# The third expert's rows asked for in the third step, the first expert's in the eighth

## The chip, the cores and the metric

One core of one Trainium2 chip runs the program. A time is device microseconds (us) of one execution; lower is better. The kernel before was timed three times, and one more execution was profiled.

## The reference

Three layers run one after the other on 3072 tokens of 384 numbers, all in float32.

```
attn:  state = alpha * state + k v^T ; y = q state          (4 x 8 heads, 768 steps, 48 wide)
moe:   h = x @ w_in ; g = h * cos(h) ; x = g @ w_out        (384 -> 2048 -> 384)
moe2:  a token with x @ w_skip > 0 goes to the expert e with the largest x @ w_gate, of 8:
       out = x + gate * (relu(x @ w1[e]) @ w2[e])           (384 -> 1024 -> 384)
       every other token: out = x
```

The change concerns the third layer, the second MoE, alone.

## The kernel before

**Stages.** Attention and the first MoE run together, in 256 half-steps, until about 588 us. The last group of tokens is routed, and then the second MoE runs, from about 602 us to the end. In it every expert has 276 slots in a table in HBM, `xs`; a slot holds a token's 384 numbers, its 8 gate logits and its row number (394 words). Tokens were scattered to their slots before.

**The second MoE.** One loop (L1008) runs over steps F = 0 to 65, eight steps for each expert (e = F // 8, f = F % 8). A step is one block of 128 of the expert's 1024 hidden numbers: `e_L1` makes the block h by nine matmuls (L958), ScalarE takes `ha` = relu(h) rounded (L961), VectorE takes `hb`, the rest of it (L962); `e_L2`, two steps later, adds the block's nine matmuls into three accumulators (L975). The tile `h` has two buffers, so the first layer of step F must wait until `hb` of step F - 2 is done.

**Loads of rows.** `e_load(e)` (L937) fetches the 276 slots of expert e into a tile `xg`: 92 partitions, three rows of 394 words on each, 425 KB, as one DMA on SyncE's queue (L939). `xg` has three buffers. An expert's rows are read three times:

- `e_T(e, k)`: three TensorE transposes each (L948), in three successive steps of the expert before it, so that the first layer can begin. For expert 1 in steps F = 5, 6 and 7, for expert 2 in steps F = 12, 13 and 14. Expert 0 needs none: its transposed rows were made in another way before the loop.
- `e_gate(e)`: the gate of its 276 tokens, five small operations on VectorE (L103, L105, L107, L109, L110) with one exponential on ScalarE (L106) in the midst. For expert 0 in step F = 9.
- `e_Y(e, j)`: VectorE multiplies the output by the gate and adds the token (L991), and GpSimd scatters it (L994). For expert 0 in steps 10, 11 and 12.

The loads of the first three experts are asked for in steps 0 (expert 1), 4 (expert 0) and 7 (expert 2); the later ones at the end of each expert, step 15 for expert 3 and so on. Here a load is called by its expert: load 1, load 0, load 2.

**Weights.** In each step `e_weights` asks for one piece of weights (L270 or L273, 384 KB on 128 partitions, tile `st`) six steps ahead of its use, and converts the piece that is due: ScalarE takes the rounded part (L287), VectorE the rest (L288). These DMAs go through the same queue of SyncE, between the loads of rows. `st` has six buffers, so SyncE waits for the conversion in the same step before it asks for the next piece.

**Order.** From half-step 246 on the order on every engine is the order of the program text (`tc.manual_schedule()`, L817); no scheduler moves anything. Inside a step it is: first layer, second layer, loads and pieces, gate, transposes of the next expert, output of the last one.

Of the kernel before, what the change touches and what calls it, by code (L numbers as in the profile page):

```python
# [19 lines left out]
DFF, E, EFF = 2048, 8, 1024  # L20
# [210 lines left out]
def linear_attention_moe_kernel(outer, tc, qk, al, v, w_in, w_out, w1, w2, idw, cst, csti, fill, q0, k0, v0, alpha0, out):  # L231
# [416 lines left out]
    with ExitStack() as order_ctx:  # L648
# [161 lines left out]
        for t in range(0, END + 2 * LAG + 1):  # L810
# [7 lines left out]
            if t >= 0:  # L818
                F, odd = divmod(t, 2)
# [84 lines left out]
        def flags1():  # L904
            ok = keep.tile([PR, 2], F32, name="ok2")
            sm = keep.tile([PR, 3], F32, name="sm")
            nc.vector.tensor_reduce(out=sm[:, 0:1], in_=amax, axis=AX.X, op=ALU.max)
            nc.vector.tensor_reduce(out=sm[:, 1:2], in_=T_all.rearrange("p n a b -> p (n a b)"), axis=AX.X, op=ALU.min)
            nc.vector.tensor_reduce(out=sm[:, 2:3], in_=run[0:PR, :], axis=AX.X, op=ALU.max)
            nc.vector.tensor_scalar(out=ok[:, 0:1], in0=sm[:, 0:1], scalar1=0.0, scalar2=None, op0=ALU.is_le)  # L910
            nc.vector.scalar_tensor_tensor(
                out=ok[:, 0:1], in0=sm[:, 1:2], scalar=T_MIN, in1=ok[:, 0:1], op0=ALU.is_ge, op1=ALU.mult
            )
            nc.vector.scalar_tensor_tensor(
                out=ok[:, 0:1], in0=sm[:, 2:3], scalar=float(CAP), in1=ok[:, 0:1], op0=ALU.is_le, op1=ALU.mult
            )
            return ok

        def flags2(ok):
            fp = tps()  # L920
            nc.tensor.matmul(fp[0:1, 0:1], ok[:, 0:1], ones_f, start=True, stop=True)
            nc.vector.tensor_scalar(
                out=flag, in0=fp[0:1, 0:1], scalar1=-1.0, scalar2=float(PR), op0=ALU.mult, op1=ALU.add
            )
# [12 lines left out]
        def e_load(e):  # L937
            x = p2.tile([ET, NJ, RW], F32, tag="xg", name="xg", bufs=3)
            nc.sync.dma_start(out=x, in_=xs[CAP * e:CAP * e + CAP, :].rearrange("(j p) d -> p j d", p=ET))  # L939
            XG[e] = x  # L940

        def e_gate(e):
            GW[e] = _gate(nc, p2, ET, NJ, XG[e][:, :, DM:DM + E], bufs=3)

        def e_T(e, k):
            pt = tps()
            for j in range(NJ):
                nc.tensor.transpose(pt[:, ET * j:ET * j + ET], XG[e][:, j, 128 * k:128 * k + 128], ident[0:ET, 0:ET])  # L948
            split_T(e, k, pt[:, 0:CAP])

        def e_L1(e, f):
            h = psh.tile([P, 512], F32, tag="h", name="h2")[:, 0:CAP]
            w = ew[e, 1]
            a, b = XT[e]
            fs = slice(128 * f, 128 * f + 128)
            k9 = [(i, x, k) for k in range(3) for i, x in ((0, a), (0, b), (1, a))]
            for n, (i, x, k) in enumerate(k9):
                nc.tensor.matmul(h, w[:, i, k, fs], x[:, k, :], start=(n == 0), stop=(n == 8))  # L958
            ha = ph[0].tile([P, CAP], F32R, tag="ha", name="ha")
            hb = ph[0].tile([P, CAP], F32R, tag="hb", name="hb")  # L960
            nc.scalar.activation(out=ha, in_=h, func=ACTF.Relu)  # L961
            nc.vector.scalar_tensor_tensor(  # L962
                out=hb, in0=h, scalar=0.0, in1=ha.bitcast(F32), op0=ALU.max, op1=ALU.subtract
            )
            H2[e, f] = (ha, hb)

        def e_L2(e, f):
            if f == 0:
                ACC[e] = [ps.tile([P, 512], F32, tag=f"acc{j}", name=f"acc{j}")[:, 0:CAP] for j in range(3)]
            w = ew[e, 2]  # L970
            a, b = H2.pop((e, f))
            for j in range(3):
                js = slice(128 * j, 128 * j + 128)
                for i, (wi, x) in enumerate(((0, a), (0, b), (1, a))):
                    nc.tensor.matmul(ACC[e][j], w[:, wi, f, js], x, start=(f == 0 and i == 0), stop=(f == NF2 - 1 and i == 2))  # L975
            if f == NF2 - 1:
                yt = p2.tile([P, 3, CAP], F32, tag="yt", name="yt")
                for j in range(3):
                    if j == 1:
                        nc.vector.tensor_copy(yt[:, j, :], ACC[e][j])  # L980
                    else:
                        nc.scalar.activation(out=yt[:, j, :], in_=ACC[e][j], func=ACTF.Copy)
                ACC[e] = yt

        def e_Y(e, j):
            pt = tps()[0:ET, 0:DM]
            for k in range(3):
                nc.tensor.transpose(pt[:, 128 * k:128 * k + 128], ACC[e][:, k, ET * j:ET * j + ET], ident)
            res = p3.tile([ET, DM], F32, tag="res", name="res")
            x = XG[e]  # L990
            nc.vector.scalar_tensor_tensor(  # L991
                out=res, in0=pt, scalar=GW[e][:, j, :], in1=x[:, j, 0:DM], op0=ALU.mult, op1=ALU.add
            )
            ins = nc.gpsimd.indirect_dma_start(  # L994
                out=out[:, :], out_offset=bass.IndirectOffsetOnAxis(ap=x[:, j, RW - 1:RW].bitcast(I32), axis=0),
                in_=res, in_offset=None, bounds_check=NTOK - 1, oob_is_err=False,
            )
            tc.declare_no_dep(ins.ins, group="rows", reason="every token has one slot")
            tc.add_to_no_dep_group("rows", ins.ins)
# [3 lines left out]
        def e_weights(i):  # L1003
            for p in pieces[i:i + 1] + pieces[i + WA:i + WA + 1]:
                next(p, None)

        tot2 = E * NF2
        for F in range(tot2 + 2):  # L1008
            e, f = divmod(F, NF2)
            if F < tot2:  # L1010
                e_L1(e, f)
            if F >= 2:
                e_L2((F - 2) // NF2, (F - 2) % NF2)
            if F < tot2:
                if F == 0:
                    e_load(1)
                e_weights(F + 4)
                if F == 4:
                    e_load(0)
                if f == FG and e or F == FG0:  # L1020
                    e_gate(e if F != FG0 else 0)
                if e + 1 < E:
                    if 0 <= f - (TF if e else TF0) < 3:
                        e_T(e + 1, f - (TF if e else TF0))
                if e >= 1 and YF <= f < YF + 3:
                    e_Y(e - 1, f - YF)
                if f == 7 and e + 2 < E:
                    e_load(e + 2)
            if F == FL1:
                ok = flags1()  # L1030
            if F == FL2:
                flags2(ok)
# [92 lines left out]
```

## Time and profile before

| | us |
|---|---|
| median of 3 runs | 785.15 |
| lowest and highest | 783.29, 785.52 |
| the profiled execution | 781.24 |
| its span, first to last instruction | 779.5 |
| busy: TensorE matmul (PE) | 742.0 (95%) |
| busy: VectorE (DVE) | 515.4 (66%) |
| busy: ScalarE (ACT) | 420.5 (54%) |
| busy: GpSimd (POOL) | 213.1 (27%) |

A row of a timeline gives the start in us, the time from the start of the first to the end of the last of the instructions that it merges, the engine, the line, the operation with what it writes and reads, how many, and in brackets how long the engine had stood idle before and what ended that. SPq is SyncE's queue, where only the issue of a DMA is seen, not its transfer. In the windows PEclk is the granted share of TensorE's 2.4 GHz: 1.00 is that level, 0.50 is 1.2 GHz.

### The profile page before, as it was taken

To read this page: it belongs to the slowest core of one execution; us is meant where nothing else is said; L and a number is where in the kernel's file an instruction comes from. 1 tells how busy PE (TensorE), PEld (TensorE's weight loads), DVE (VectorE), ACT (ScalarE), POOL (GpSimd) and SP (SyncE) were. 2 spreads that over 40 slices of the span, in tenths; PEclk is the share of its full clock that TensorE was granted. 3 is DMA by queue.
4 is the path that set the end of the run, shared out by engine and by line. 5 is a ranking of instruction groups with operands and counts; after the bars stand their busy time and mean duration, and the time that the engine had idled before them with its cause. 6 is when DMAs were issued, how large, how long until landed. Compare 5 with 4: busy or idle time off the path is not lost.

```text
span 779.5 us, 13544 instructions
## 1 busy us (share of the span) xinstructions
PE 742.0 (95%) x5033; PEld 725.8 (93%) x5033; DVE 515.4 (66%) x1088; ACT 420.5 (54%) x877; POOL 213.1 (27%) x217
## 2 busy tenths in 40 slices
PE   6689999999999999999999999999999989999995
PEld 4689899989999999999999999999998989999994
DVE  5889999986676656667756544444444667777772
ACT  3789996454454454455445445535554545555551
POOL 3003324232524224222422322232342021111112
PEclk7979999999999999999999999999999999999998
DMA  9858772421233222213322210102033766666621
GB/s 274 272 186 267 232 251 85 147 94 34 72 115 99 84 95 85 68 52 114 100 84 90 75 60 16 51 22 87 31 100 108 195 164 195 196 182 188 199 65 27
DMA packets 53217, 94.77 MB, mean 122 GB/s; under 512 B 7950, under 2 KB 39265, under 8 KB 53048
## 3 DMA queue, kind: packets, MB, share of 16 engines
q1 hardware_dynamic: 47528, 88.82, 37.5%
q0 software_dynamic: 4992, 4.80, 2.1%
q8 instruction: 41, 0.67, 0.4%
q10 hardware_dynamic: 624, 0.21, 0.1%
q14 instruction: 32, 0.26, 0.1%
HBM read 82.03 MB, written 16.43 MB: 126 GB/s over the span
## 4 chain that ended last, share of the span: by engine, by line
PE 60%; issue 16%; DVE 6%; POOL 3%; DMA 2%; ACT 1%; POOLq 0%; SPq 0%; ACTq 0%
PE acc L570 24%; PE h L535 22%; PE sc L438 4%; POOL out L994 3%; PE y L448 2%; PE y L451 2%; DMA xg<-xs 2%; PE u L494 1%; PE y L454 1%; DVE w L398 1%; PE h L958 1%; DVE w L409 1%; PE pt L429 1%; PE wg L323 1%; DVE n L539 1%
## 5 line engine op out<-in xcount | busy, mean ns | idle before, releaser
L556 POOL TENSOR_TENSOR gl<-n,gh 128x384 fp32r<-128x384 f32 x127 | 140.2, 1104 | 334.9 <-ACT gh L554 247.8
L535 PE MATMUL h<-x,win_h 128*128 128x384 f32 x768 | 204.6, 347 | 7.7 <-ACT x L474 5.8
L535 PEld LDWEIGHTS h<-x,win_h 128*128 128x128 f32 x768 | 137.8, 191 | 9.4 <-ACT x L474 6.0
L570 PE MATMUL acc<-wout_h,gh 128*128 128x394 f32 x384 | 136.7, 356 | 0.0
L570 PE MATMUL acc<-wout_h,gl 128*128 128x394 f32 x384 | 132.0, 344 | 0.4 <-POOL gl L556 0.4
L570 PE MATMUL acc<-wout_l,gh 128*128 128x394 f32 x384 | 132.2, 344 | 0.0
L535 PE MATMUL h<-x,win_l 128*128 128x384 f32 x384 | 130.8, 341 | 0.0
L546 ACT ACTIVATE n<-n,lims 128x384 f32<-128x384 f32 x128 | 78.9, 616 | 89.1 <-DVE n L539 89.0
L539 DVE SCALAR_TENSOR_TENSOR n<-n,h 128x384 f32<-128x384 int32 x128 | 70.1, 548 | 83.7 <-ACT n L538 82.8
L554 ACT ACTIVATE gh<-n 128x384 fp32r<-128x384 f32 x128 | 67.0, 523 | 72.7 <-DVE n L547 72.3
L547 DVE TENSOR_TENSOR n<-n,h 128x384 f32<-128x384 f32 x128 | 70.4, 550 | 50.9 <-ACT n L546 50.3
L538 ACT ACTIVATE n<-h 128x384 int32<-128x384 f32 x128 | 62.3, 487 | 54.4 <-PE h L535 48.4
L958 PE MATMUL h<-xt,w1t 128*128 128x276 f32 x576 | 88.2, 298 | 0.3 <-DVE xt L871 0.3
L975 PE MATMUL acc<-ha,w2t 128*128 128x276 f32 x384 | 83.5, 290 | 0.0
L958 PEld LDWEIGHTS h<-xt,w1t 128*128 128x128 f32 x576 | 77.7, 191 | 0.9 <-DVE xt L871 0.7
L570 PEld LDWEIGHTS acc<-wout_h,gl 128*128 128x128 f32 x384 | 72.7, 189 | 0.7 <-POOL gl L556 0.7
L535 PEld LDWEIGHTS h<-x,win_l 128*128 128x128 f32 x384 | 73.2, 191 | 0.0
L570 PEld LDWEIGHTS acc<-wout_h,gh 128*128 128x128 f32 x384 | 72.8, 190 | 0.3 <-ACT gh L554 0.3
L570 PEld LDWEIGHTS acc<-wout_l,gh 128*128 128x128 f32 x384 | 72.7, 189 | 0.0
L994 POOL DMA_INDIRECT out<-res,xg x24 | 29.7, 1238 | 141.3 <-DVE res L991 137.2
L975 PEld LDWEIGHTS acc<-ha,w2t 128*128 128x128 f32 x384 | 64.6, 189 | 0.0
L961 ACT ACTIVATE ha<-h 128x276 fp32r<-128x276 f32 x64 | 25.6, 400 | 58.2 <-PE h L958 57.9
(148 smaller groups left out, 1229.4 us busy)
## 6 DMA issues: line engine op xcount, KB each, us to landing
st<-w SPq DMA_DIRECT2D x64, 384.0 KB
v<-v SPq DMA_DIRECT2D x24, 576.0 KB
qk<-qk SPq DMA_DIRECT2D x24, 448.0 KB
w<-al SPq DMA_DIRECT2D x22, 462.0 KB
st<-w_in SPq DMA_DIRECT2D x16, 384.0 KB
st<-w_out SPq DMA_DIRECT2D x16, 384.0 KB
out<-R SPq DMA_DIRECT2D x6, 576.0 KB
xs<-fill SPq DMA_DIRECT2D x8, 424.8 KB
```

What stands on the lines that cost most here:

```text
L438: nc.tensor.matmul(sc[:, p, :], KB[:, 1 - i, p, :], QK[n][:, 0, p, 64 * i:128], start=True, stop=True)
L535: nc.tensor.matmul(h, a[:, k, fs], X[g][:, i, k, :], start=(n == 0), stop=(n == 8))
L538: nc.scalar.activation(out=n, in_=h, func=ACTF.Copy, scale=1.0 / TWO_PI, bias=0.25)
L539: nc.vector.scalar_tensor_tensor(out=u, in0=n, scalar=-TWO_PI, in1=h, op0=ALU.mult, op1=ALU.add)
L546: nc.scalar.activation(out=u, in_=u, func=ACTF.Sin, bias=quarter)
L547: nc.vector.tensor_tensor(out=u, in0=u, in1=h, op=ALU.mult)
L554: nc.scalar.activation(out=a, in_=u, func=ACTF.Copy)
L556: eng.tensor_tensor(out=b, in0=u, in1=a.bitcast(F32), op=ALU.subtract)
L570: nc.tensor.matmul(acc[g][j][:, 0:WC], x[:, js], w[:, f, :], start=(f == 0 and i == 0), stop=(f == NF - 1 and i == 2))
L958: nc.tensor.matmul(h, w[:, i, k, fs], x[:, k, :], start=(n == 0), stop=(n == 8))
L975: nc.tensor.matmul(ACC[e][j], w[:, wi, f, js], x, start=(f == 0 and i == 0), stop=(f == NF2 - 1 and i == 2))
L994: ins = nc.gpsimd.indirect_dma_start(out=out[:, :], out_offset=bass.IndirectOffsetOnAxis(ap=x[:, j, RW - 1:RW].bitcast(I32), axis=0), in_= ...
```

## The change

Two of the three first loads of rows trade places in the program: load 2 is asked for in the third step (F = 2) instead of the eighth, load 0 in the eighth (F = 7) instead of the fifth. No instruction is added or removed. The third line keeps the later loads as they were.

```diff
                 e_weights(F + 4)
-                if F == 4:
+                if F == 2:
+                    e_load(2)
+                if F == 7:
                     e_load(0)
                 if f == FG and e or F == FG0:
                     e_gate(e if F != FG0 else 0)
...
-                if f == 7 and e + 2 < E:
+                if f == 7 and 0 < e < E - 2:
                     e_load(e + 2)
```

On SyncE's queue the loads stand among the pieces of weights. Before, from the first step of the second MoE on (`xg_6274` is load 1, `xg_6384` load 0, `xg_6486` load 2):

```order
L939 DMA xg_6274<-xs_72 92x3x394
L273 DMA st_6279<-w1 128x3x256
L273 DMA st_6297<-w1 128x3x256
L270 DMA st_6327<-w2 128x2x384
L270 DMA st_6354<-w2 128x2x384
L270 DMA st_6382<-w2 128x2x384
L939 DMA xg_6384<-xs_72 92x3x394
L270 DMA st_6411<-w2 128x2x384
L273 DMA st_6445<-w1 128x3x256
L273 DMA st_6478<-w1 128x3x256
L939 DMA xg_6486<-xs_72 92x3x394
L273 DMA st_6514<-w1 128x3x256
```

Now, in the same place (`xg_6274` is load 1, `xg_6329` load 2, `xg_6480` load 0):

```order
L939 DMA xg_6274<-xs_72 92x3x394
L273 DMA st_6279<-w1 128x3x256
L273 DMA st_6297<-w1 128x3x256
L270 DMA st_6327<-w2 128x2x384
L939 DMA xg_6329<-xs_72 92x3x394
L270 DMA st_6356<-w2 128x2x384
L270 DMA st_6384<-w2 128x2x384
L270 DMA st_6411<-w2 128x2x384
L273 DMA st_6445<-w1 128x3x256
L273 DMA st_6478<-w1 128x3x256
L939 DMA xg_6480<-xs_72 92x3x394
L273 DMA st_6514<-w1 128x3x256
```

The middle load has moved ahead of two pieces and is now that of expert 2; the last load stands where the last one stood, behind the same eight pieces and two loads, and is now that of expert 0.

VectorE's order is the same but for the DMA that its gate of expert 0 (L103) waits for; its place in step F = 9, as a piece of the difference (`yt` is the output of expert 0, `w2t` the converted piece):

```order
 L980 COPY yt<-acc_6314 128x276 [waits PE_49]
-L288 TENSOR_TENSOR w2t<-st,w2t 128x768 [waits DMAHW5_49,Activation_49]
-L103 TENSOR_REDUCE gm<-xg 92x3 [waits DMAHW7_49]
+L288 TENSOR_TENSOR w2t<-st,w2t 128x768 [waits DMAHW6_49,Activation_49]
+L103 TENSOR_REDUCE gm<-xg 92x3 [waits DMAHW3_49]
 L105 TENSOR_TENSOR gd<-xg,gm 92x24 [waits DVE_49]
 L107 TENSOR_REDUCE gm<-gd 92x3 [waits Activation_49]
```

The gate waits for load 0 as before, under another semaphore; it has not moved, while the load that it waits for has.

## Rows read from the trace of the kernel before

**Rows 1.** The page: span, and busy time of TensorE.
```profile
span 779.5 us, 13544 instructions
PE 742.0 (95%) x5033; PEld 725.8 (93%) x5033; DVE 515.4 (66%) x1088; ACT 420.5 (54%) x877; POOL 213.1 (27%) x217
```

**Rows 2.** Waits of TensorE, 600 to 780 us: total, times, longest.
```profile
PE tp L948 <- DMA xg<-xs: 3.7, 2, 3.0
```

**Rows 3.** Timeline of TensorE, steps 5 to 13 of the second MoE.
```profile
614.42 0.43 PE L948 MATMUL tp<-idw_sb,xg 92*128 92x92 f32 x3 [0.21 <-issue]
...
629.89 0.49 PE L988 MATMUL tp<-idw_sb,yt 128*92 128x128 f32 x3
630.13 1.39 PE L958 MATMUL h<-xt,w1t 128*128 128x276 f32 x9
...
635.70 0.56 PE L948 MATMUL tp<-idw_sb,xg 92*128 92x92 f32 x3 [3.04 <-DMA xg<-xs]
...
636.56 2.42 PE L958 MATMUL h<-xt,w1t 128*128 128x276 f32 x9
```

**Rows 4.** Timeline of SyncE's queue, issues of loads and pieces.
```profile
605.30 0.29 SPq L939 DMA_DIRECT2D xg<-xs  x1
606.02 1.59 SPq L273 DMA_DIRECT2D st<-w  x2
608.47 4.89 SPq L270 DMA_DIRECT2D st<-w  x3
613.41 0.36 SPq L939 DMA_DIRECT2D xg<-xs  x1
615.27 0.88 SPq L270 DMA_DIRECT2D st<-w  x1
618.22 2.94 SPq L273 DMA_DIRECT2D st<-w  x2
621.21 0.41 SPq L939 DMA_DIRECT2D xg<-xs  x1
```

**Rows 5.** Chain of waits, load 0: start, duration, what.
```profile
613.41 12.63 DMA xg<-xs
626.04 0.02 issue
```

**Rows 6.** Timeline of VectorE, steps 9 to 11.
```profile
626.35 0.96 DVE L288 TENSOR_TENSOR w2t<-st,w2t 128x768 fp32r<-128x768 f32 x1 [1.09 <-ACT w2t L287]
627.23 0.17 DVE L103 TENSOR_REDUCE gm<-xg 92x3 f32<-92x24 f32 x1
...
628.40 0.41 DVE L962 SCALAR_TENSOR_TENSOR hb<-h,ha 128x276 fp32r<-128x276 f32 x1
628.92 0.96 DVE L288 TENSOR_TENSOR w2t<-st,w2t 128x768 fp32r<-128x768 f32 x1
629.79 0.61 DVE L991 SCALAR_TENSOR_TENSOR res<-tp,gw,xg 92x384 f32<-92x384 f32 x1
630.32 0.43 DVE L962 SCALAR_TENSOR_TENSOR hb<-h,ha 128x276 fp32r<-128x276 f32 x1
```

**Rows 7.** Timeline of ScalarE, steps 9 and 10.
```profile
625.48 0.84 ACT L287 ACTIVATE w2t<-st 128x768 fp32r<-128x768 f32 x1
627.64 0.22 ACT L106 ACTIVATE gd<-gd 92x24 f32<-92x24 f32 x1 [1.32 <-DVE gd L105]
627.77 0.38 ACT L961 ACTIVATE ha<-h 128x276 fp32r<-128x276 f32 x1
```

**Rows 8.** Timeline of TensorE, its two longest idle times before the first MoE.
```profile
12.85 1.01 PE L429 MATMUL pt<-idw_sb,qk 112*128 112x112 f32 x4 [5.54 <-DVE qk L416]
...
40.32 1.54 PE L535 MATMUL h<-x,win_h 128*128 128x384 f32 x3 [5.82 <-ACT x L474]
```

**Rows 9.** Windows: stretch, length, busy time of PE, PEld, DVE, ACT, POOL (instructions), clock, DMA.
```profile
11.00:21.00 10.00, 7.65 (x38) 7.31 (x38) 5.05 (x12) 5.38 (x10) 3.40 (x4) 0.51 1.04 354
38.60:48.70 10.10, 8.38 (x31) 8.03 (x32) 9.79 (x20) 8.48 (x22) 0.21 (x1) 0.50 0.42 149
...
635.70:639.30 3.60, 3.60 (x18) 3.58 (x19) 1.76 (x8) 0.69 (x2) 1.18 (x1) 0.53 0.53 195
639.30:642.70 3.40, 3.40 (x29) 3.40 (x29) 2.20 (x4) 2.19 (x5) 0.00 (x0) 1.00 0.27 64
642.70:772.00 129.30, 126.68 (x1015) 125.59 (x1013) 89.17 (x175) 64.74 (x132) 22.48 (x20) 1.00 0.54 157
```

## The prediction

> **What bounds the kernel now.** I read the page first, then TensorE's waits, then the timelines of the four engines around the one long wait, then the windows for the clock. TensorE is busy 742.0 of 779.5 us [rows 1], and behind the place of the change, from 642.7 to 772 us, 126.68 of 129.30 us [rows 9]. So the second MoE is bound by TensorE, and a delay or a gain of TensorE near 630 us goes on to the end unshortened. In the whole second MoE TensorE waits 3.7 us for loads of rows, in two places, 3.0 of it in one [rows 2]: in step F = 12 the first transposes of expert 2 stand 3.04 us and start at 635.70 [rows 3], when load 2 has landed. Behind that wait the clock is granted 0.53 for 3.6 us, the 1.2 GHz level for most of it, and 1.00 again after 639.3 [rows 9]; nine matmuls take 2.42 us at 636.56 and took 1.39 at 630.13 [rows 3]. The stall therefore costs 3.04 us, and 3.6 x (1 - 0.53) = 1.7 us in speed: 4.7 us together. That is all that the change can remove, for the other wait, 0.7 us, is of a later load.
>
> **When the loads land.** They are issued at 605.30, 613.41 and 621.21 [rows 4]. Load 1 has landed by 614.42, when its transposes start after an idle time of 0.21 [rows 3]; load 0 lands at 626.04 [rows 5]; load 2 at 635.6, just before the transposes of 635.70. That is 9.1, 12.6 and 14.4 us after the issue: a load does not take a time of its own, it stands behind what was asked for earlier. Take the queue as served in order, with p us for a piece and L for a load. Between the landings of load 1 and load 0 lie five pieces and a load (two of L273, three of L270) [rows 4]: 5p + L = 626.0 - 614.4 = 11.6. Between load 0 and load 2 lie three pieces and a load: 3p + L = 635.6 - 626.0 = 9.6. So p = 1.0 and L = 6.6 us. Load 1 alone, with 9.1 us from issue to landing, fits: 6.6 and 2.5 for the latency at both ends. A load of 425 KB thus costs more than six times what a piece of 384 KB does.
>
> The Trainium skill ("DMA: Bandwidth & Descriptors", section "Why a DMA increments its semaphore by 16 and not by 1") says that a DMA runs on the largest number of engines up to 16 that divides its slowest dimension: 16 for the 128 partitions of a piece, but 4 for the 92 of a load, always the lowest-numbered ones. By that an estimate of a load is 4 x 1.0 x 425/384 = 4.6 us, where the landings give 6.6, and it would put load 2 at 622 instead of 624 us in the changed kernel; the landing of the last load in the queue, which decides, stays where it is.
>
> **The change part by part.** *Load 2 in the third step.* It now stands behind load 1 and three pieces: 614.4 + 3 x 1.0 + 6.6 = 624.0 us. TensorE wants it at 632.7, the 635.70 less the 3.04 [rows 3]. The stall goes, with 8 us to spare: -3.0 us, and -1.7 us of clock.
>
> *Load 0 in the eighth step.* It is issued where load 2 was, at 621.2, and stands behind the same eight pieces and two loads. Only their order differs, so it lands when load 2 did: 624.0 + 5 x 1.0 + 6.6 = 635.6 us. The gate of expert 0 wants it on VectorE at 627.23 [rows 6]; before, load 0 had landed 1.2 us earlier. VectorE now stands there for about 8.4 us, and ScalarE with it, since the exponential (L106) stands ahead of `ha` of step 10 on ScalarE [rows 7]. Queued behind the gate on VectorE are `hb` of step 10, a piece, the first output, `hb` of step 11 [rows 6]. From the start of the gate to the end of `hb` it took 628.81 - 627.23 = 1.6 us; with 0.1 for the semaphores `hb` of step 10 is done at 637.3. TensorE has one step of room: the first layer of step 11 needs `hb` of step 9, done long before, but that of step 12 needs the buffer that `hb` of step 10 releases. It started at 630.13, behind transposes (L988) that end at about 630.3 [rows 3]. So TensorE stands from 630.3 to 637.3: +7.0 us.
>
> *The clock behind the new stall.* No row shows an idle time of 7 us. The nearest are 3.04 us, with 3.6 us at 1.2 GHz after it, and 5.54 and 5.82 us ahead of 12.85 and 40.32 [rows 8], in whose wake the clock stays at 0.51 and 0.50 until 21 and 48.7 [rows 9], some 8.3 us after TensorE resumed. From below: the slow stretch ends where it ended before, at 639.3, and costs half of 639.3 - 637.3, 1.0 us. From above: 8.3 us, or a little more, after the resumption, half of it 4.2 us. I take 2.7, near the middle, since the early stretches had further idle time in them (PE 7.65 of 10.00 and 8.38 of 10.10 us) [rows 9].
>
> *What is late next.* Behind `hb` of step 10 VectorE has 0.96 + 0.61 + 0.43 = 2.0 us to the end of `hb` of step 11 [rows 6], some overlap left out: 639.3. The first layer of step 13 wants it after step 12's two layers, 2.6 us at full and more at the low clock, so from 639.9 on. VectorE catches up in time and this costs nothing; without that cover it would be 1 to 2 us. The piece that follows load 2 lands at 624.0 + 1.0 = 625.0 or a little later and is converted at 625.48 [rows 7]: up to 1 us of lateness on ScalarE, hidden behind the gate's wait. SyncE waits for VectorE's conversions in steps 10 and 11 and asks for pieces about 8 us later than now; they are due six steps on, some 15 us, when the queue's backlog is gone: 0.
>
> *The sum*, against the profiled execution: -3.0 - 1.7 + 7.0 + 2.7 = +5.0 us, 781.24 to 786.2. That execution lies 3.9 us below the median of the runs, 785.15; the median goes to 790.1, said as 790. The unknown clock alone gives 788.4 to 791.6.
>
> **The rivals.** *The load runs from its own issue* (faster). If the queue does not serve in order, load 0, issued at 621.2, lands after a load's own time: 6.6 us, so 627.8, and TensorE does not stand at all, since `hb` is then done at 629.5; or the 9.1 us of load 1, so 630.3, `hb` at 632.0 and a stall of 1.7 us. The gain is then 4.7 us, or 3.0 with an untouched clock: 780.4 to 782.2. The deciding point is a landing before 631.6, where the new stall is as long as the old one. Against it: 12.6 and 14.4 us for loads 0 and 2, which it does not explain. The Trainium skill ("DMA: Bandwidth & Descriptors", section "Queues, rings and completion order") speaks for it in so far as it says that completion is not in the order of issue across the engines; by the sharing of the same lowest four engines, its other rule, it would not help a load behind loads.
>
> *The two stalls cancel* (no change). If load 0 lands between 631 and 632.5, say because the engines that carry loads had idle time between them that the new order fills, the new stall is 2.4 to 3.9 us and the clock's loss the same as before: 784.5 to 786. For it: the middle load is asked for some 4 us earlier. Against it: the landings at p = 1.0 leave no gap to fill, since issues run ahead of landings by 9 us and more.
>
> *VectorE and ScalarE don't catch up* (slower still). The 2.0 us and the next 2.0 us of work behind `hb` of step 10, with the flags of step 12, keep the buffers of h for another 1 to 2 us: 791.5 to 792.5. For it: VectorE has all of this to do in two steps of TensorE. Against it: TensorE runs these two steps at the low clock.
>
> **How the numbers follow.** The forecast has 0.76, the early landing 0.09, the cancelling stalls 0.10, the missing catch-up 0.05. A measurement of this kernel can tell about 0.3%, 2.4 us, from no change. Slower by more than that: the forecast but for the part that a short slow stretch and the spread of the runs (2.2 us between lowest and highest) bring down, 0.73, and the missing catch-up, 0.05: 0.78. Within it: 0.10 and 0.03 from the forecast, 0.13. Faster: 0.09. The forecast's own range is 787 to 792.5; 784.5 to 793 takes in the cancelling stalls and the missing catch-up and leaves out the early landing and tails, some 0.15.
>
> **What would show it.** In the profile after: the transposes of expert 2 without idle time in step 12; the gate of expert 0 starting at about 635.7 with some 8 us of idle time of VectorE ahead of it, ended by the load; TensorE idle for about 7 us ahead of the first layer of step 12, and not of transposes; the clock at 0.5 for 2 to 9 us behind it; the span near 784.5. The prediction is wrong if load 0 lands before 631.6 us, or if the order in the queue lets TensorE find other work.

## The result, and the profile after

The changed kernel takes 787.13 us (median of 20 runs, 783.96 to 791.07), the kernel before 782.60 (20 runs, 779.27 to 785.52). The ratio is 1.0060, with a 95% interval of 1.0044 to 1.0076: slower by 4.7 us (3.4 to 5.9). The prediction said +5.0 us, 784.5 to 793.0 us. The three runs of before that were known then lay high, at 785.15, so the forecast of 790.0 stands 2.9 us above the time while the difference is right within 0.3 us.

The profiled execution has a span of 785.0 us, 5.5 more than before. Not all of it is the change's: the second MoE begins at 604.42 here and at 602.17 before, by the first row of L958 on TensorE's timeline (before, then after). In three further executions of the kernel before, that start lies between 598.7 and 603.0, so that it moves without any change.

```profile
602.17 4.04 PE L958 MATMUL h<-xt,w1t 128*128 128x276 f32 x27
604.42 4.07 PE L958 MATMUL h<-xt,w1t 128*128 128x276 f32 x27
```

From there to the end it is 180.6 us against 177.3: +3.3 us. Times below that are compared with those of before are 2.25 us later for this reason alone.

TensorE's waits from 600 us on (the columns are total, times, longest; before, [rows 2]):

```profile
PE h L958 <- DVE hb L962: 6.8, 1, 6.8
PE ft L893 <- DVE sel L885: 0.7, 1, 0.7
PE tp L948 <- DMA xg<-xs: 0.4, 1, 0.4
PE h L958 <- DVE xt L871: 0.3, 1, 0.3
```

TensorE no longer waits 3.0 us for load 2; it waits 6.8 us, once, for `hb`. What remains for a load is the later wait of 0.7 us, now 0.4. The wait of 0.7 us at L893 belongs to the routing ahead of the second MoE and stands in every kernel here. The timeline of TensorE shows where the new wait stands (before, [rows 3]):

```profile
632.11 0.49 PE L988 MATMUL tp<-idw_sb,yt 128*92 128x128 f32 x3
639.41 2.44 PE L958 MATMUL h<-xt,w1t 128*128 128x276 f32 x9 [6.80 <-DVE hb L962]
...
643.14 0.40 PE L948 MATMUL tp<-idw_sb,xg 92*128 92x92 f32 x3
643.37 0.49 PE L988 MATMUL tp<-idw_sb,yt 128*92 128x128 f32 x3
643.62 1.39 PE L958 MATMUL h<-xt,w1t 128*128 128x276 f32 x9
```

The stall sits between the output transposes of step 11 and the first layer of step 12. The transposes of expert 2 follow at 643.14 without an idle time, and so does the first layer of step 13. VectorE tells why `hb` was late (before, [rows 6]):

```profile
629.04 0.96 DVE L288 TENSOR_TENSOR w2t<-st,w2t 128x768 fp32r<-128x768 f32 x1 [1.56 <-ACT w2t L287]
637.77 0.17 DVE L103 TENSOR_REDUCE gm<-xg 92x3 f32<-92x24 f32 x1 [7.76 <-DMA xg<-xs]
...
638.94 0.41 DVE L962 SCALAR_TENSOR_TENSOR hb<-h,ha 128x276 fp32r<-128x276 f32 x1
...
640.86 0.43 DVE L962 SCALAR_TENSOR_TENSOR hb<-h,ha 128x276 fp32r<-128x276 f32 x1
```

The gate of expert 0 stands 7.76 us for load 0, and `hb` of step 10 comes 1.6 us behind its start, as before. ScalarE stands in the same way, its exponential waiting 9.17 us, and the piece behind load 2 is converted 0.36 us late:

```profile
628.16 0.85 ACT L287 ACTIVATE w2t<-st 128x768 fp32r<-128x768 f32 x1 [0.36 <-DMA st<-w]
638.18 0.22 ACT L106 ACTIVATE gd<-gd 92x24 f32<-92x24 f32 x1 [9.17 <-DVE gd L105]
```

SyncE's queue (before, [rows 4]) and the chain of waits (before, [rows 5]) give the time of the load itself:

```profile
607.50 0.29 SPq L939 DMA_DIRECT2D xg<-xs  x1
...
611.17 0.36 SPq L939 DMA_DIRECT2D xg<-xs  x1
...
623.43 1.42 SPq L939 DMA_DIRECT2D xg<-xs  x1
```
```profile
623.43 14.32 DMA xg<-xs
```

Load 0, asked for at 623.43, lands 14.3 us later, at 637.75. Less the 2.25 us that is 635.5, and load 2 landed at 635.6 in the kernel before: the last of the three loads lands when the last one did, whosever rows it carries. The chain goes on from this landing, through the five operations of the gate and `hb`, to the first layer of step 12 without a gap.

The windows show the clock behind the stall (length, busy PE, PEld, DVE, ACT, POOL, clock, DMA share, GB/s; before, [rows 9]):

```profile
635.70:639.30 3.60, 0.00 (x0) 0.00 (x0) 1.14 (x6) 1.11 (x3) 0.00 (x0) 0.50 0.25 85
639.30:642.70 3.40, 3.29 (x15) 3.29 (x16) 3.29 (x7) 1.90 (x5) 1.46 (x1) 0.54 0.33 105
642.70:646.10 3.40, 3.40 (x31) 3.40 (x30) 3.25 (x11) 1.83 (x4) 2.79 (x3) 1.00 0.73 200
```

The clock had fallen to 1.2 GHz while TensorE still stood. What it cost is in the second window alone: 3.3 us of matmuls at 0.54, some 1.5 us.

### The profile page after: what moved, and what is told of

Its sections match the earlier page's. It is cut to its first block, busy times and chain, and to the rows that moved or that the text cites. A ratio compares the mean times of both kernels' runs of the same rounds, so it can differ in the third digit from the quotient of the medians.

```text
span 785.0 us, 13544 instructions
## 1 busy us (share of the span) xinstructions
PE 741.0 (94%) x5033; PEld 725.1 (92%) x5033; DVE 516.7 (66%) x1088; ACT 419.6 (53%) x877; POOL 210.6 (27%) x217
## 4 chain that ended last, share of the span: by engine, by line
PE 59%; issue 15%; DVE 7%; POOL 3%; DMA 2%; ACT 1%; POOLq 0%; SPq 0%; ACTq 0%
PE acc L570 23%; PE h L535 21%; PE sc L438 4%; POOL out L994 3%; PE y L448 2%; PE y L451 2%; DMA xg<-xs 2%; PE h L958 2%; PE u L494 1%; PE y L454 1%; DVE w L398 1%; DVE w L409 1%; PE acc L975 1%; DVE n L539 1%; PE pt L429 1%
## 5 line engine op out<-in xcount | busy, mean ns | idle before, releaser
L958 PE MATMUL h<-xt,w1t 128*128 128x276 f32 x576 | 88.3, 299 | 7.1 <-DVE hb L962 6.8
L958 PEld LDWEIGHTS h<-xt,w1t 128*128 128x128 f32 x576 | 77.9, 192 | 7.8 <-DVE hb L962 7.1
```

## The experiments

The kernels of the first four were timed together, against 781.97 us of the kernel before on that chip; the next four together, against 780.83; the last three runs of this section are one profiled execution each. The diffs are excerpts; a line `...` marks what is left out.

| kernel | us | ratio to before, 95% | difference, us |
|---|---|---|---|
| load 2 early only | 783.19 | 1.0016 (0.9996 to 1.0037) | +1.3 (-0.3 to +2.9) |
| load 0, then load 2 | 778.85 | 0.9953 (0.9928 to 0.9978) | -3.7 (-5.6 to -1.7) |
| split 80 + 12, old order | 776.13 | 0.9929 (0.9903 to 0.9954) | -5.6 (-7.6 to -3.6) |
| split 80 + 12, new order | 776.70 | 0.9929 (0.9901 to 0.9958) | -5.6 (-7.7 to -3.3) |
| gate in step 13 | 779.00 | 0.9976 (0.9950 to 1.0002) | -1.9 (-3.9 to +0.2) |
| matmuls in the stall | 784.38 | 1.0053 (1.0023 to 1.0082) | +4.1 (+1.8 to +6.4) |
| split 46 + 46, old order | 837.74 | 1.0730 (1.0688 to 1.0772) | +57 (+54 to +60) |
| the changed kernel again | 786.30 | 1.0068 (1.0043 to 1.0092) | +5.3 (+3.4 to +7.2) |

**One part of the change alone.** Against the kernel before; the third line of the change stays in, here and in the next experiment.

```diff
-                if F == 4:
+                if F == 2:
+                    e_load(2)
+                if F == 4:
                     e_load(0)
```

> Load 2 is asked for in step 2 as in the change, load 0 stays in step 4: one part of the change alone. In-order queue (a piece 1.0 us, a load 6.6 us): load 2 lands at 624, load 0 two pieces and a load later, at 632.6 in the time base of the kernel before, though it is asked for at 613.4 as before; the gate of expert 0 stands about 5 us, TensorE about 4 us ahead of the first layer of step 12, and the stall of the transposes of step 12 is gone: 0 to +2 us against the kernel before. If a load ran from its own issue, load 0 would land at about 622.5 to 626, no stall would be left: -4.7 us.

It came out in the range of the in-order queue: +1.3 us, not told from no change, and not -4.7. TensorE's waits, the issue of load 0 and VectorE's gate:

```profile
PE h L958 <- DVE hb L962: 3.3, 1, 3.3
```
```profile
615.83 1.06 SPq L939 DMA_DIRECT2D xg<-xs  x1
```
```profile
632.30 0.17 DVE L103 TENSOR_REDUCE gm<-xg 92x3 f32<-92x24 f32 x1 [4.73 <-DMA xg<-xs]
```

Load 0 is asked for in the same step as in the kernel before, though SyncE comes to it 2.2 us later, and lands 6 us later: at 632.3, or 632.1 in the time base of before, where the in-order queue had 632.6 and a load's own time 626 at most. From its own issue it takes 16.4 us instead of 12.6, now that load 2 stands ahead of it. The early place of load 2 alone is enough to make the gate wait; the later place of load 0 adds the rest.

**The same two places, experts traded.**

```diff
-                if F == 4:
+                if F == 2:
                     e_load(0)
+                if F == 4:
+                    e_load(2)
```

> Load 0 in step 2, load 2 in step 4: the same two places in the queue as in the experiment before, with the experts traded. In-order queue: load 0 lands at 624.0, 3 us before its gate wants it (627.2); load 2 lands at 632.6, just when its transposes want it (632.7). Neither stall is left, or a few tenths of a us: -4 to -5 us against the kernel before, about -9 against the changed one. If the loads' time came from something else than their place in the queue, for example from a bandwidth shared by all that is in flight, load 2 would be late here as in the kernel before: -1 to +1 us.

-3.7 us, as an in-order queue has it, and not the -1 to +1 of a shared bandwidth. In the profile neither the gate nor the transposes of step 12 wait for a load:

```profile
631.91 0.17 DVE L103 TENSOR_REDUCE gm<-xg 92x3 f32<-92x24 f32 x1
```
```profile
637.30 0.43 PE L948 MATMUL tp<-idw_sb,xg 92*128 92x92 f32 x3
```

It has a wait elsewhere, at the first transposes of expert 1 ("issue" means that the profile names nothing that ended it):

```profile
619.13 0.43 PE L948 MATMUL tp<-idw_sb,xg 92*128 92x92 f32 x3 [2.79 <-issue]
```

That is load 1, which only the kernels that split the loads change; it returns below.

**A load on more engines.** Each load of rows becomes two DMAs, in the old order of loads and in the new:

```diff
-            nc.sync.dma_start(out=x, in_=xs[CAP * e:CAP * e + CAP, :].rearrange("(j p) d -> p j d", p=ET))
+            rows = xs[CAP * e:CAP * e + CAP, :].rearrange("(j p) d -> p j d", p=ET)
+            nc.sync.dma_start(out=x[0:80], in_=rows[0:80])
+            nc.sync.dma_start(out=x[80:ET], in_=rows[80:ET])
```

> The kernel before, with every load of rows issued as two DMAs, of partitions 0 to 79 and 80 to 91; the order of the loads as before. If a load is slow because 92 partitions go to 4 of 16 DMA engines (80 go to 16 and 12 to 12, by the rule of the Trainium skill), a load costs about 6.6 x 18/69 = 1.7 us instead of 6.6, every load lands well before it is wanted, and both waits for loads (3.7 us) and the slow clock (1.7 us) go: -5 us. If a load is slow for its bytes or its short rows, nothing changes: 0 us.

> The changed kernel with the same split of every load. If the four engines are the cause, load 0, asked for at 621.2 in the time base of the kernel before, lands some 4 to 6 us later, at 625 to 627.5, about when the gate wants it: no stall of TensorE, -5 us against the kernel before, equal to the split kernel with the old order within 1 us. If not, the gate stands as in the changed kernel: +4.7 us.

Both give -5.6 us, and with short loads the order of the change no longer matters: 776.13 and 776.70 us. In the profile of the split kernel with the new order load 0 is asked for at 620.47 and 621.00, and the gate waits 0.22 us:

```profile
620.47 0.48 SPq L940 DMA_DIRECT2D xg<-xs  x1
621.00 0.42 SPq L941 DMA_DIRECT2D xg<-xs  x1
```
```profile
626.77 0.17 DVE L103 TENSOR_REDUCE gm<-xg 92x3 f32<-92x24 f32 x1 [0.22 <-DMA xg<-xs]
```

So with every load split this one takes 5.8 us from its second issue, not 14.3. These two kernels are the fastest of all. The Trainium skill ("DMA: Bandwidth & Descriptors", section "Why a DMA increments its semaphore by 16 and not by 1") has the rule that chose 80 and 12: the largest number of engines up to 16 that divides the slowest dimension. The runs agree with it, and the next one more so, by their times; no trace here shows which engines carried a load.

**Two DMAs of 46.** Against the split kernel with the old order:

```diff
-            nc.sync.dma_start(out=x[0:80], in_=rows[0:80])
-            nc.sync.dma_start(out=x[80:ET], in_=rows[80:ET])
+            nc.sync.dma_start(out=x[0:46], in_=rows[0:46])
+            nc.sync.dma_start(out=x[46:ET], in_=rows[46:ET])
```

> The kernel before, with every load of rows issued as two DMAs of 46 partitions each, instead of one of 92 or of 80 and 12. If two DMAs in place of one are what helps, the time is that of the split kernel: -5 us. If the number of engines is what counts (46 partitions go to 2 engines by the rule of the Trainium skill, both halves to the same two), a load takes twice as long, 13 us: load 1 lands about 6 us late for its transposes, load 0 about 12 us late for its gate, load 2 about 20 us late, less what the earlier stalls give back: +15 to +25 us.

+57 us: two DMAs in place of one are not what helped. 46 can be divided by 2 and 23, so that by the same rule of the Trainium skill both halves go to the same two engines. The size, +15 to +25, was missed: the expectation counted the three first loads, and the loads of all seven experts that are transposed in the loop are late. TensorE waits for them 46.5 us in all, and the mean clock of the span falls to 0.945.

```profile
PE tp L950 <- DMA xg<-xs: 40.9, 6, 11.0
PE tp L950 <- issue: 5.6, 1, 5.6
```

**The gate out of the way.** Against the changed kernel: its loads, with the gate of expert 0 and its outputs moved behind the landing:

```diff
-YF, TF, TF0, FG, FG0, FL1, FL2 = 2, 4, 5, 6, 9, 12, 17
+YF, TF, TF0, FG, FG0, FL1, FL2 = 2, 4, 5, 6, 13, 12, 17
...
-            x = p2.tile([ET, NJ, RW], F32, tag="xg", name="xg", bufs=3)
+            x = p2.tile([ET, NJ, RW], F32, tag="xg", name="xg", bufs=4)
...
-                if e >= 1 and YF <= f < YF + 3:
-                    e_Y(e - 1, f - YF)
+                y0 = YF if e > 1 else YF + 3
+                if e >= 1 and y0 <= f < y0 + 3:
+                    e_Y(e - 1, f - y0)
```

> The changed kernel with the gate of expert 0 in step 13 instead of 9 and its three outputs in steps 13 to 15 instead of 10 to 12; the tile of rows gets a fourth buffer so that load 3 need not wait for those outputs. The order of the loads is that of the change. If the changed kernel is slow because the gate stands on VectorE ahead of work that TensorE needs, then here load 0, landing at 635.6, is in time for a gate at about 635, no stall is left: -4 to -5 us against the kernel before, -8 to -10 against the changed one. If load 0 is late by so much that it delays other things itself, or the queue's backlog delays the pieces, the time stays at +3 to +5 us.

The new stall is gone: 779.0 us, 7.3 below the changed kernel on the same chip, where 8 to 10 were expected. Load 0 lands late as before, and the gate, in step 13, waits 0.69 us with no stall of TensorE behind it:

```profile
636.72 0.17 DVE L103 TENSOR_REDUCE gm<-xg 92x3 f32<-92x24 f32 x1 [0.69 <-DMA xg<-xs]
```

So the late load costs only by way of the gate and what is queued behind it on VectorE. (The fourth buffer of `xg` was not tried alone.) Against the kernel before it is -1.9 us (-3.9 to +0.2), less than the 4 to 5 expected; the paragraph on the old stall has a reason.

**The clock behind the stall.** In the changed kernel TensorE is given matmuls whose result nobody reads:

```diff
                     e_Y(e - 1, f - YF)
+                if F == 11:
+                    hp = tps()
+                    for _ in range(110):
+                        nc.tensor.matmul(hp[:, 0:128], ones, ones, start=True, stop=True)
```

> The changed kernel with 110 matmuls of 128 x 128 in bfloat16, whose result nobody reads, behind the output transposes of step 11, where TensorE stands 6.8 us; they take about 6 us at the full clock and change nothing for the other engines. What they take away is the slow clock behind the stall: 1.5 us in the profile of the changed kernel, 2.7 in the prediction. So -1.5 us against the changed kernel, or -2.7; with a clock that does not fall behind an idle engine, 0.

In the profile they fill 6.30 us of the stall, and the clock stays at 1.00, where the changed kernel run beside it has 0.50 (the first layer of step 12 takes 1.41 us, there 2.44):

```profile
630.56 6.30 PE L1032 MATMUL tp<-ones 128*128 128x128 bf16 x110
636.90 1.41 PE L958 MATMUL h<-xt,w1t 128*128 128x276 f32 x9
```
```profile
630.00:633.00 3.00, 3.00 (x51) 2.99 (x50) 0.00 (x0) 0.00 (x0) 0.00 (x0) 1.00 0.58 177
633.00:636.00 3.00, 3.00 (x58) 3.00 (x56) 0.42 (x3) 0.33 (x2) 0.00 (x0) 1.00 0.29 100
636.00:639.00 3.00, 2.97 (x32) 2.80 (x30) 2.82 (x8) 2.54 (x6) 0.26 (x1) 1.00 0.08 23
```

> The changed kernel itself, on the chip of the three others, as their measure: +4.7 us against the kernel before. Its profile shows again a stall of TensorE of 6 to 7 us ahead of the first layer of step 12, ended by hb, and the gate's wait of about 8 us on VectorE; the slow clock behind it may last more or less than the 3.0 us seen.

```profile
615.44 0.43 PE L948 MATMUL tp<-idw_sb,xg 92*128 92x92 f32 x3 [2.99 <-issue]
...
638.06 2.44 PE L958 MATMUL h<-xt,w1t 128*128 128x276 f32 x9 [6.64 <-DVE hb L962]
```
```profile
636.50:638.00 1.50, 0.00 (x0) 0.00 (x0) 1.11 (x6) 1.16 (x4) 0.00 (x0) 0.50 0.20 67
638.00:641.00 3.00, 2.94 (x13) 2.94 (x14) 2.89 (x6) 1.51 (x5) 1.11 (x1) 0.50 0.28 89
641.00:643.00 2.00, 2.00 (x18) 2.00 (x18) 1.92 (x4) 1.13 (x2) 1.70 (x2) 0.97 0.65 180
```

The changed kernel repeats itself: a stall of 6.64 us and 3 us of matmuls at half speed behind it, 1.5 us. It also shows a wait of 2.99 us for load 1 that its first profile did not have. The times, 784.38 and 786.30, differ by 1.9 us, but their intervals overlap, so that the clock's price is shown by the profiles and not by the times: about 1.5, not 2.7.

**How steady the old stall is.** The kernel before, unchanged, was profiled three more times.

> The kernel before, once more with a profile, to see how steady the size of the old stall is. If the stall of the transposes of step 12 always costs what it cost in the first profile, it shows 3.0 us of idle time and a clock near 0.5 for about 3.5 us behind it, 4.7 us in all. If the fall of the clock depends on chance, the stall is there (2.5 to 3.5 us) with the clock left at 1.00, and the change took away 3 us only, which makes the +4.7 of the comparison out of +3.3 in the profiles.

The other two were given the same expectations: "

> As the run before: a second look at the same kernel, for the idle time of TensorE ahead of the transposes of step 12 and the clock behind it; 3.0 us and 0.5 if it is steady, a clock of 1.00 if it is chance.

" and "

> As the two runs before: a third look at the same kernel, with the same expectations.

".

It is not steady, and not in its clock alone. In the first of the three TensorE stands at two places, for load 1 in step 5 and for load 2 in step 12, and behind the second the clock stays at 1.00:

```profile
612.78 0.43 PE L948 MATMUL tp<-idw_sb,xg 92*128 92x92 f32 x3 [2.06 <-issue]
```
```profile
633.49 0.43 PE L948 MATMUL tp<-idw_sb,xg 92*128 92x92 f32 x3 [2.47 <-DMA xg<-xs]
```
```profile
632.00:636.00 4.00, 2.51 (x22) 2.54 (x23) 1.68 (x8) 0.98 (x3) 1.51 (x2) 1.00 0.78 232
636.00:640.00 4.00, 4.00 (x36) 4.00 (x35) 3.14 (x7) 2.10 (x4) 0.83 (x1) 1.00 0.50 157
```

In the second there is no wait for load 1, and 0.81 us for load 2; in the third 3.60 us for load 1, with a slow clock behind it, and none for load 2:

```profile
634.37 0.43 PE L948 MATMUL tp<-idw_sb,xg 92*128 92x92 f32 x3 [0.81 <-DMA xg<-xs]
```
```profile
616.07 0.43 PE L948 MATMUL tp<-idw_sb,xg 92*128 92x92 f32 x3 [3.60 <-issue]
```
```profile
616.00:620.00 4.00, 3.94 (x20) 3.96 (x21) 1.29 (x3) 1.53 (x3) 0.00 (x0) 0.58 0.61 190
```

Over four profiles the old stall is 3.04, 2.47, 0.81 and 0 us, 1.6 in the mean, with a slow clock behind it in one, 0.4 in the mean: 2 us in all. That fits a gain of 1.9 us with the gate out of the way, and +1.3 us with load 2 early alone, where a stall of 3.3 us takes its place. The split loads, which end the wait for load 1 too, gain most.

The wait for load 1 goes by the time of its issue. SyncE asks for it when the last scatter of tokens into `xs` has landed; in its queue that is a wait of 8.7 us in the first profile of the kernel before, 10.0 in the third of the further ones and 10.6 in the changed kernel's second. The issues in the last two:

```profile
606.26 0.29 SPq L939 DMA_DIRECT2D xg<-xs  x1
```
```profile
606.75 0.29 SPq L939 DMA_DIRECT2D xg<-xs  x1
```

Here are the six profiles of the two kernels from the start of the second MoE, in us. "Slow clock" is the matmul time in the slow stretch times what the clock lacked of 1.00.

| profile | load 1 issued after the start | wait for load 1 | for load 2 or `hb` | for a later load | slow clock | length | length less all these |
|---|---|---|---|---|---|---|---|
| before | 3.1 | 0.2 | 3.0 | 0.7 | 1.7 | 177.3 | 171.7 |
| before, second | 4.4 | 2.1 | 2.5 | 0 | 0 | 176.5 | 172.0 |
| before, third | 2.7 | 0 | 0.8 | 0 | 0 | 172.8 | 172.0 |
| before, fourth | 5.8 | 3.6 | 0 | 0.5 | 1.7 | 177.1 | 171.3 |
| changed | 3.1 | 0 | 6.8 | 0.4 | 1.5 | 180.6 | 171.9 |
| changed, second | 6.4 | 3.0 | 6.6 | 0 | 1.5 | 182.6 | 171.5 |

Where TensorE waits for load 1, here and in the other kernels with whole loads, its transposes start 8.7 to 9.8 us after the issue: a late issue is a late landing. What is left when all waits and the clock are taken off is 171.3 to 172.0 us in all six; the two split kernels, which have none of these waits, take 171.2 and 171.1.

## Why the prediction was right

*The queue in order*: right, and the step on which the sign hung. The last load lands at 635.5 in the time base of before, for 635.6 foretold; with load 0 three pieces earlier in the queue it lands at 632.1, for 632.6; with the experts traded both stalls end. The rival in which a load runs from its own issue would have shown -4.7 us for the early load 2 alone, and that kernel was not faster.

*Load 2 in time*: right. Its transposes start without idle time, and the piece behind it is late by 0.36 us of the "up to 1" and hidden.

*The gate and the stall*: right. VectorE waited 7.8 us for 8.4 foretold, TensorE 6.8 for 7.0, at the place named; with the gate in step 13 the stall is gone while the load is as late as ever.

*What is late next*: nothing, as said. `hb` of step 11 ends at 641.3, the first layer of step 13 starts at 643.62 with no wait.

*The clock behind the new stall*: too large. It measured 1.5 us in two profiles for the 2.7 taken; it lies in the foretold 1.0 to 4.2, near its lower end.

*What the change removes*: too large as well, and the weakest step. "That is all that the change can remove" was right as an upper end, 4.7 us, but the sum took it whole, from one execution. Four profiles have 1.6 us of stall and 0.4 of clock in the mean, 2 us.

These two go against each other. With the measured sizes the sum is 6.7 + 1.5 - 2.0 = +6.2 us, from two profiles of the changed kernel and four of the one before; the times say +4.7 (3.4 to 5.9). The foretold +5.0 is so near partly by luck: two wrong sizes cancelled. The profiles themselves add up. For the first pair the stalls and the clock of the table give +3.1 us, and the second MoE is 3.3 longer. In the means of four and two it is 175.9 and 181.6 us, +5.7: load 1 waits 1.5 us in both means, but in the kernel before the clock fell behind one such wait, 0.4 us in the mean, and the sum of 6.2 left that out. Between 5.7 and 4.7 stand six profiles against forty runs, of kernels whose waits differ by 3 us and more from one execution to the next.

*A slip*: the rival without catch-up adds 1 to 2 us to the forecast of 790, which is 791 to 792 and not "791.5 to 792.5". Nothing hung on it.

## What to carry to other kernels

Where a queue has a backlog, the place of a request in it counts more than the moment at which it is asked for; load 1, with nothing just ahead of it, landed by its issue. So read the landing times of several requests, fit a cost for each kind, and add up what stands ahead of the one that is wanted first. Order requests by when they are wanted, and look at which engine waits: the same late load cost TensorE nothing when its reader stood late in VectorE's order, and 6.8 us when work for TensorE was queued behind that reader. Before reordering slow requests, see whether they can be made short: splitting 92 partitions into 80 and 12 gained 5.6 us, the best order of the loads 3.7. And a stall read from one profile is one draw; here it was between 0 and 3 us, and four profiles with the length of the stage beside them showed where the rest had gone.

## What the runs showed of the hardware

- Every load of 92 partitions made into two DMAs of 80 and 12 cut the last load's time from issue to landing from 14.3 to 5.8 us in the same place of the program; two of 46 cost 57 us.
- Stalls of TensorE of 3.04 and 3.60 us were followed by a clock of 0.53 and 0.58, in two profiles of the kernel before; those of 2.06 and 2.47 in another of its profiles, of 2.99 in the changed kernel and of 3.30 in the kernel with load 2 early (below, its clock around the stall) were followed by 1.00. The length of a stall alone did not decide it, and one kernel differed by up to 1.7 us from one execution to the next for the clock alone.

```profile
630.00:633.00 3.00, 0.64 (x6) 0.38 (x4) 0.38 (x3) 0.28 (x2) 0.00 (x0) 1.00 0.68 180
633.00:636.00 3.00, 2.06 (x16) 2.06 (x17) 2.83 (x8) 2.54 (x6) 0.22 (x1) 1.00 0.30 90
636.00:639.00 3.00, 3.00 (x27) 3.00 (x27) 3.00 (x6) 1.75 (x4) 2.69 (x2) 1.00 0.80 210
```
